# A long convolution beside a feed-forward block on one core: tying the order of TensorE's two streams to the program's, moving loads of the last stage, and a longer pause ahead of it

## The chip, the core and the metric

The kernel runs on one core of a Trainium2 chip. The metric is the device time of one execution in microseconds; the kernel before was run three times: 1074.57, 1076.01 and 1077.52 us, median 1076.01. A separate, profiled execution gives the trace that is read here.

The engines are named as the profile has them: PE is TensorE's matmuls and PEld its weight loads, DVE is VectorE, ACT is ScalarE, POOL is GpSimd, and SP is SyncE, which issues most of the DMAs (SPq, its queue). Each engine works through its own instructions in the order in which the built program has them. L685 is line 685 of the kernel's file.

## What is computed

The reference adds three parts for a sequence of 2048 rows and 576 columns (cut here to what matters):

```python
x = A_q
xn = layernorm(x)
k_shift = sum of 4 shifted k, each times shift_k     # short causal convolution
kv = k_shift * v
y = irfft(rfft(kv, 4096) * rfft(ssm_k, 4096))[:2048] # long causal convolution, per column
y = y + kv * ssm_D
ffn = relu(xn @ w1) @ w2                              # 576 -> 4608 -> 576
return x + xn * y + ffn
```

## The kernel before

Two streams of work share the engines, and both need TensorE.

**The feed-forward block (FFN)** goes through 18 pairs of 128-wide slices of the hidden width, twice: the first half of the program for rows 0 to 1023, the second half for the others. A visit computes the hidden values of 512 rows (`mm1`, L559, in the first half; `quad`, L587, in the second, with fewer products and more sums, whose partial results go through ScalarE and VectorE and back into PSUM) and puts them through `relu` (tiles `hh` and `ll`, the high and low part of each value, by ScalarE and VectorE). A `unit` (L616) multiplies hidden values by the second weights into a PSUM tile `pso`; VectorE adds it to `acc` (L636, L640). Units wait in a list, and `fill` takes two size units of them (24 matmuls) after each stage of a visit. GpSimd splits weights (`split_lo`, L426).

**The convolution (conv)** is a transform by matrices in four stages, written as a generator, `conv` (L694), which hands control back after each piece of work:

- fk: 64 steps transform `ssm_k`. For a step, VectorE transposes a block (`tr`, L758, one for two steps), ScalarE and VectorE split it into the stacked operand `ks` (L678, L679), TensorE multiplies it by `wk` (two matmuls, L685), ScalarE copies the result (`zk`, L686) and a DMA stores it. `ks`, `wk` and the copies have three buffers each.
- fx: 64 steps do the same for the gated `k * v`, with operands `xs` that are put together by DMAs (L839).
- fm: 192 steps, the middle of the transform and the product of both spectra; it ends with stores into `zy`.
- fo: 64 steps transform back, four for each of 16 row tiles. Each two steps need a load `zo` of 576 KB from `zy` (L991; four buffers, asked for three loads ahead). For each row tile, `load_rest` (L994) loads the matrix `wi` (GpSimd's queue, L998), the rows `xt` (L160) and, for half of the tiles, the FFN's finished sums `ft` (L1004, two buffers). `gate` and `add` (L1012, L1020) combine them on VectorE.

**What sets the order.** While the program is written out, each group of FFN matmuls calls `tick` with its columns (the moving operand's width, a measure of TensorE's work). `tick` lets the conv generator go on when its share is due: each piece has a cost (`W_FK`, `W_FX`, `W_FM`, `W_FO`) and `rate` spreads all of them over the FFN's columns; a negative yield is a pause of so many columns. That gives the program's order. But the built order on each engine is made by a scheduler that plays the program through with its own durations: whenever an engine is free, it takes the earliest instruction of the program whose operands are ready by its reckoning. So an FFN matmul can go ahead of a conv step that stands earlier in the program, and the other way round. `tc.issue_after(a)` forbids that for the instructions inside the block: on their engine they come behind `a`. It adds no wait on a semaphore; it only fixes an order. `here` (L689) uses it for conv's work on VectorE and ScalarE. Nothing used it for matmuls.

Of the kernel before, what the change touches and what calls it, by code (L numbers as in the profile page):

```python
# [10 lines left out]
F32 = mybir.dt.float32  # L11
# [6 lines left out]
P = 128  # L18
S = 2048
D = 576  # L20
# [3 lines left out]
NH = D // 2  # L24
# [10 lines left out]
HT = T // HALVES  # L35
# [25 lines left out]
W_QUAD = sum(W_STAGE)  # L61
FFN_TOTAL = NPAIR * HB * (W_PLAIN + W_QUAD + 2 * 4 * W_UNIT)
# [47 lines left out]
def h3_ffn_kernel(ctx: ExitStack, tc, x, k, v, shift_k, ssm_k, ssm_D, w1, w2, fwd, inv, mid, out):  # L110
    nc = tc.nc
# [35 lines left out]
    acc = {}  # L147
# [52 lines left out]
    done = {}  # L200
# [339 lines left out]
    def bank(m, name):  # L540
        return ps_h.tile([P, 512], F32, tag=f"h{m}", name=name)

    def run_seq(ps, seq, start=False):
        for i, (a, m) in enumerate(seq):
            nc.tensor.matmul(ps, a, m, start=start and i == 0, stop=i == len(seq) - 1,  # L545
                             skip_group_check=not start)

    def relu(n, s, j, ps):
        hh = hp.tile([P, 512], F32R, tag="hh", name=f"hh{n}_{s}_{j}")
# [10 lines left out]
    def mm1(n, s, j):  # L560
        g = weights[n][j]
        ps = bank(j, f"psh{n}_{s}_{j}")
        seq = []
        for c in range(4):
            b = ops[s, "b2" if c % 2 else "b1"][:, :, c // 2]
            seq += [(g[:, 0, c], b[:, 0]), (g[:, 0, c], b[:, 1]), (g[:, 1, c], b[:, 0])]
        seq += rest(n, j, s)
        for i, (a, m) in enumerate(seq):
            nc.tensor.matmul(ps, a, m, start=i == 0, stop=i == len(seq) - 1)  # L569
            if i % 7 == 6:  # L570
                tick(W_PLAIN / 4)
        relu(n, s, j, ps)
# [42 lines left out]
    def unit(ns, s, b, i, h, last):  # L615

        t = b * BT + i
        cols = slice(i * P, (i + 1) * P)
        final = b >= HB and last
        if final:  # L620
            while t not in added:
                next(stream)
        ps = ps_o.tile([P, 512], F32, tag="o", name=f"pso{ns[0]}_{t}_{h}")
        dc = slice(h * NH, (h + 1) * NH)
        seq = []
        for n in ns:
            for j in range(FT):
                hh, ll = hid[n, s, j]
                w = weights[n]["w2", h][:, :, j]
                seq += [(hh[:, cols], w[:, 0]), (hh[:, cols], w[:, 1]), (ll[:, cols], w[:, 0])]  # L630
        for c, (a, m) in enumerate(seq):
            nc.tensor.matmul(ps[:, :NH], a, m, start=c == 0, stop=c == len(seq) - 1)  # L632
            if c % 6 == 5:
                tick(6 * NH)
        if b == 0:
            done["acc"] = nc.vector.scalar_tensor_tensor(  # L636
                acc[t][:, dc], ps[:, :NH], rstd[:, t:t + 1], acc[t][:, dc],
                op0=OP.mult, op1=OP.add)
        else:
            done["acc"] = nc.vector.tensor_tensor(acc[t][:, dc], ps[:, :NH], acc[t][:, dc],  # L640
                                                  OP.add)
# [39 lines left out]
    def first(w, stk, z, u):  # L681

        ps = fft_psum()
        for n in range(2):
            nc.tensor.matmul(ps[:, :NH], w[:, n, :], stk, start=n == 0, stop=n == 1)  # L685
        nc.scalar.activation(z, ps[:, :NH], AF.Copy)  # L686

    @contextmanager
# [6 lines left out]
    def conv():  # L695
# [179 lines left out]
        with tc.tile_pool(name="fm", bufs=2) as fp:  # L875
# [22 lines left out]
            def run(hi, lo, d, h):  # L898

                ps = fft_psum()  # L900
                cols = slice(h * NH, (h + 1) * NH)
                seq = [(m_sb[:, d, 0, :], hi), (m_sb[:, d, 0, :], lo), (m_sb[:, d, 1, :], hi)]
                for n, (a, m) in enumerate(seq):
                    nc.tensor.matmul(ps[:, :NH], a, m[:, cols], start=n == 0, stop=n == 2)
                return ps[:, :NH], cols

            load(zk, 0, "k")
# [69 lines left out]


        with tc.tile_pool(name="fo", bufs=2) as fp:
            parts, rest, ys = {}, {}, {}  # L980


            order = [*range(HT, T), *range(HT)]
# [10 lines left out]
            def load_rest(i):  # L994
                if i < T:
                    t = order[i]
                    w = fp.tile([P, U, P], F32R, tag="wt", name=f"wi{t}", bufs=3)
                    nc.gpsimd.dma_start(w, inv[t])  # L998
                    xt = fp.tile([P, D], F32, tag="xt", name=f"xt{t}", bufs=3)
                    move(xt, x, t)  # L1000
                    ft = None
                    if t < HT:
                        ft = fp.tile([P, D], F32, tag="ft", name=f"ft{t}", bufs=2)
                        nc.sync.dma_start(ft, fin[t // 2, :, t % 2, :])  # L1004
                    rest[i] = w, xt, ft

            def gate(i):

# [6 lines left out]
            def add(i):  # L1015
                if i >= 0:
                    t = order[i]
                    to, more = (ys[i], rest[i][2]) if t < HT else (acc[t], acc[t])
                    with here():
                        nc.vector.scalar_tensor_tensor(to, ys[i], rstd[:, t:t + 1], more,  # L1020
                                                       op0=OP.mult, op1=OP.add)
# [6 lines left out]
                load_z(n)  # L1028
            for i in range(2):
                load_rest(i)  # L1030
            yield -2 * PAUSE
            for n, (t, u) in enumerate(units):
                i = n // U
                w = rest[i][0]
# [5 lines left out]
                for h in range(2):  # L1040


                    ps = fft_psum()
                    cols = slice(h * NH, (h + 1) * NH)
                    nc.tensor.matmul(ps[:, :NH], w[:, u, :], hi[:, cols], start=True, stop=False)  # L1045
                    nc.tensor.matmul(ps[:, :NH], w[:, u, :], lo[:, cols], start=False, stop=True)  # L1046
# [194 lines left out]
```

## Time and profile before

| what | value |
|---|---|
| median of 3 runs | 1076.01 us |
| the profiled execution's own time | 1079.17 us |
| its span, first to last instruction | 1077.4 us |
| TensorE busy | 1054.3 us, 98% |
| VectorE, ScalarE, GpSimd busy | 742.6, 549.6, 396.9 us |
| mean granted clock of TensorE | 0.994 |
| DMA | 204.45 MB, 190 GB/s |
| fk steps on TensorE | 82.4 to 205.4 us |
| fx steps | 238.6 to 503.3 us |
| fo steps | 891.5 to 1042.9 us |

A busy TensorE in this profile is one with a matmul under way; what counts is where it is not, and what ended that. A view by stretches gives, for each stretch of time, the busy time of each engine, the number of instructions, the granted clock (1.00 is full), the DMA engines' busy share and GB/s. The waits name the instruction that waited, what it waited for, the total, how often, and the longest. The chain is followed back from the last instruction through whatever released each step.

### The profile page before, as it was taken

The numbers are of one execution on the slowest core, as the hardware profiler recorded it, in microseconds if no ns is written. First come the engines' busy times: TensorE is split into PE (matmuls) and PEld (weight loads), VectorE is DVE, ScalarE is ACT, GpSimd is POOL, SyncE is SP. The second block draws the span as 40 slices with busy tenths as digits, with TensorE's granted clock in tenths as the row PEclk, the third lists the DMA queues.
The fourth block names the chain that finished last, engine by engine and source line by source line (L and its number), as shares of the span: only waits on it lengthen the run. The fifth ranks groups of instructions, "written<-read, shape, count | busy, mean of one in ns | idle before, by whom it ended". The sixth has DMA issues, their size and how long they took to land. (4 is left out here: it accounts for less than half of the span.)

```text
span 1077.4 us, 20001 instructions
## 1 busy us (share of the span) xinstructions
PE 1054.3 (98%) x7153; PEld 992.8 (92%) x7153; DVE 742.6 (69%) x1314; ACT 549.6 (51%) x1201; POOL 396.9 (37%) x398
## 2 busy tenths in 40 slices
PE   8999999999899999999999999999999998999998
PEld 5889999998799999999999999999999998999897
DVE  4539778779686878752487778777877755665654
ACT  4226556434433444432477787778677753443330
POOL 4133333232223233334343544434343444444531
PEclk9999999999999999999999999999999999999999
DMA  8845867778756766856875565566565559766824
GB/s 205 199 95 143 221 174 212 196 220 213 207 175 173 200 157 194 249 154 199 292 226 183 175 176 178 168 190 179 168 192 143 156 167 317 235 222 198 265 67 110
DMA packets 156303, 204.45 MB, mean 190 GB/s; under 512 B 32845, under 2 KB 122703, under 8 KB 155180
## 3 DMA queue, kind: packets, MB, share of 16 engines
q1 hardware_dynamic: 143308, 189.00, 59.3%
q0 software_dynamic: 12576, 13.44, 5.6%
q8 instruction: 56, 0.92, 0.4%
q10 hardware_dynamic: 320, 0.74, 0.3%
q14 instruction: 43, 0.35, 0.1%
HBM read 133.92 MB, written 55.05 MB: 175 GB/s over the span
## 5 line engine op out<-in xcount | busy, mean ns | idle before, releaser
L632 PE MATMUL pso<-w,hh 128*128 128x288 f32 x2304 | 470.5, 295 | 1.6 <-ACT w L531 0.8
L632 PEld LDWEIGHTS pso<-w,hh 128*128 128x128 f32 x2304 | 373.7, 188 | 10.3 <-ACT w L531 1.2
L632 PE MATMUL pso<-w,ll 128*128 128x288 f32 x1152 | 328.1, 295 | 0.0
L427 POOL TENSOR_TENSOR g<-r,g 128x256 fp32r<-128x256 f32 (+2 forms) x145 | 169.4, 1174 | 385.0 <-ACT g L469 343.8
L569 PE MATMUL psh<-b,g 128*128 128x512 f32 x864 | 218.9, 397 | 0.5 <-ACT b L223 0.2
L632 PEld LDWEIGHTS pso<-w,ll 128*128 128x128 f32 x1152 | 212.9, 188 | 1.0
L569 PEld LDWEIGHTS psh<-b,g 128*128 128x128 f32 x864 | 158.1, 189 | 31.1 <-DVE b L224 0.5
L640 DVE TENSOR_TENSOR acc<-pso,acc 128x288 f32<-128x288 f32 x232 | 102.3, 450 | 73.8 <-PE pso L632 72.8
L427 POOL TENSOR_TENSOR w<-r,w 128x576 fp32r<-128x576 f32 x72 | 115.2, 1601 | 57.8 <-ACT w L531 57.6
L551 ACT ACTIVATE hh<-psh 128x512 fp32r<-128x512 f32 x72 | 42.9, 597 | 127.1 <-PE psh L569 127.0
L552 DVE SCALAR_TENSOR_TENSOR ll<-psh,hh 128x512 fp32r<-128x512 f32 x72 | 49.3, 685 | 69.2 <-ACT hh L551 68.7
L545 PE MATMUL psb<-t,g 128*128 128x256 f32 x648 | 95.8, 281 | 0.0
L469 ACT ACTIVATE g<-r 128x256 fp32r<-128x256 f32 (+2 forms) x145 | 76.2, 542 | 33.6 <-DMA r<-in_w 25.4
L545 PEld LDWEIGHTS psb<-t,g 128*128 128x128 f32 x648 | 86.2, 189 | 0.1
L498 POOL TENSOR_TENSOR r<-r 128x256 f32<-128x256 f32 x72 | 58.0, 826 | 37.4 <-DMA r<-in_w 36.1
L545 PE MATMUL psa<-b,g 128*128 128x256 f32 x432 | 63.0, 281 | 0.4 <-ACT psa L596 0.4
L545 PE MATMUL psb<-b,g 128*128 128x256 f32 x432 | 59.6, 284 | 0.0
L545 PEld LDWEIGHTS psa<-b,g 128*128 128x128 f32 x432 | 56.6, 188 | 0.6 <-ACT psa L596 0.6
L545 PEld LDWEIGHTS psb<-b,g 128*128 128x128 f32 x432 | 56.0, 192 | 0.1
L672 POOL DMA_DIRECT2D wx<-in_fwd x32 | 17.7, 555 | 96.8 <-PE psf L685 85.6
L551 ACT ACTIVATE hh<-psa 128x512 fp32r<-128x512 f32 x36 | 21.6, 599 | 58.0 <-PE psa L545 57.7
L636 DVE SCALAR_TENSOR_TENSOR acc<-pso,rstd,acc 128x288 f32<-128x288 f32 x72 | 36.4, 510 | 20.1 <-PE pso L632 19.6
(134 smaller groups left out, 1693.7 us busy)
## 6 DMA issues: line engine op xcount, KB each, us to landing
r<-in_w SPq DMA_DIRECT2D x72, 288.0 KB, 3.6
zy<-vo SPq DMA_DIRECT2D x64, 288.0 KB, 3.1
zo<-zy SPq DMA_DIRECT2D x32, 576.0 KB, 5.8
r<-in_w SPq DMA_DIRECT2D x35, 512.0 KB, 4.5
zk<-zk SPq DMA_DIRECT2D x64, 144.0 KB, 2.5
ztk<-zk SPq DMA_DIRECT2D x32, 288.0 KB, 3.2
ztx<-zx SPq DMA_DIRECT2D x32, 288.0 KB, 3.1
k<-k SPq DMA_DIRECT2D x64, 144.0 KB, 3.2
```

The source lines that it names most:

```text
L427: return nc.gpsimd.tensor_tensor(dst, src, hi, OP.subtract)
L469: nc.scalar.activation(hi, src, AF.Copy)
L498: nc.gpsimd.tensor_tensor(dst, a, b, op)
L545: nc.tensor.matmul(ps, a, m, start=start and i == 0, stop=i == len(seq) - 1, skip_group_check=not start)
L551: done["act"] = nc.scalar.activation(hh, ps, AF.Relu)
L552: lows.append(nc.vector.scalar_tensor_tensor(ll, ps, 0.0, hh, op0=OP.max, op1=OP.subtract))
L569: nc.tensor.matmul(ps, a, m, start=i == 0, stop=i == len(seq) - 1)
L632: nc.tensor.matmul(ps[:, :NH], a, m, start=c == 0, stop=c == len(seq) - 1)
L636: done["acc"] = nc.vector.scalar_tensor_tensor(acc[t][:, dc], ps[:, :NH], rstd[:, t:t + 1], acc[t][:, dc], op0=OP.mult, op1=OP.add)
L640: done["acc"] = nc.vector.tensor_tensor(acc[t][:, dc], ps[:, :NH], acc[t][:, dc], OP.add)
L672: nc.gpsimd.dma_start(w, src)
```

## The change

1. **The order of matmuls.** Conv's matmuls in fk, fx, fm and fo now stand behind the last FFN matmul that was written before them (`done["pe"]`). FFN matmuls stand behind the newest conv step that is at least `LAG` = 4000 FFN columns old (`in_turn`). So an FFN matmul may pass a conv step by about 4000 columns, and a conv step passes no FFN matmul that was the last one written. FFN matmuls keep their freedom among themselves. Since `tick` comes every 1728 to 4096 columns, the limit is met in such pieces.
2. **Loads of fo.** `load_rest(i + 2)` is called one step later (in the first step of a tile's second half, instead of the second of its first half). The load of `ft` leaves it and becomes `load_sum(i)`, for the tile at hand instead of two tiles ahead; it is called behind the `add` of two tiles before, which frees its buffer.
3. **The pause ahead of fo** is 13/4 of 16,000 columns instead of 2; the sum of all pauses, `PAUSES`, grows by the same 1.25, so the rest of conv runs at a rate that is 1.2% higher.

```diff
+LAG = 4000
-PAUSES = 4 * NH // Q // KB * KT_GAP / PAUSE + 14
+PAUSES = 4 * NH // Q // KB * KT_GAP / PAUSE + 15.25
...
+    steps = []
+
+    def in_turn():
+
+        before = clock["ffn"] - LAG
+        while len(steps) > 1 and steps[1][0] <= before:
+            steps.pop(0)
+        if steps and steps[0][0] <= before:
+            return tc.issue_after(steps[0][1].ins)
+        return nullcontext()
+
+    def step(ins):
+        steps.append((clock["ffn"], ins))
...
         for i, (a, m) in enumerate(seq):
-            nc.tensor.matmul(ps, a, m, start=i == 0, stop=i == len(seq) - 1)
+            with in_turn():
+                done["pe"] = nc.tensor.matmul(ps, a, m, start=i == 0, stop=i == len(seq) - 1)
...
     def first(w, stk, z, u):
 
         ps = fft_psum()
-        for n in range(2):
-            nc.tensor.matmul(ps[:, :NH], w[:, n, :], stk, start=n == 0, stop=n == 1)
+        with tc.issue_after(done["pe"].ins):
+            for n in range(2):
+                last = nc.tensor.matmul(ps[:, :NH], w[:, n, :], stk, start=n == 0, stop=n == 1)
+        step(last)
         nc.scalar.activation(z, ps[:, :NH], AF.Copy)
...
-                    ft = None
-                    if t < HT:
-                        ft = fp.tile([P, D], F32, tag="ft", name=f"ft{t}", bufs=2)
-                        nc.sync.dma_start(ft, fin[t // 2, :, t % 2, :])
-                    rest[i] = w, xt, ft
+                    rest[i] = w, xt
+
+            def load_sum(i):
+                t = order[i]
+                if t < HT:
+                    sums[i] = fp.tile([P, D], F32, tag="ft", name=f"ft{t}", bufs=2)
+                    nc.sync.dma_start(sums[i], fin[t // 2, :, t % 2, :])
...
-            yield -2 * PAUSE
+            yield -13 * PAUSE / 4
...
                     if h == 0:
                         load_z(n + 3)
+                        if u:
+                            load_rest(i + 2)
                     else:
                         (gate if u == 0 else add)(i - 1)
                         if u == 0:
-                            load_rest(i + 2)
+                            load_sum(i)
                     yield W_FO
```

The matmuls of `run_seq`, `unit`, fm (`run`) and fo are wrapped in the same way.

What this does to the built order is shown at three places. The number at a name's end counts tiles in the order in which the program asks for them; the same tile has nearly the same number in both kernels. `psh` is the PSUM tile of `mm1`, `psa` and `psb` are those of `quad`, `pso` that of a unit, `psf` that of a conv step. First, TensorE in fk, before, where conv's step for `ks5_1` stands:

```order
L569 MATMUL psh4_0_1_1535<-xr_0_369,g4_2_1368 128x512 x2
L632 MATMUL pso2_2_1_1576<-w2_2_1_945,hh2_1_0_772 128x288
L685 MATMUL psf_1318<-ks5_1_1285,wk10_1214 128x288 x2
L632 MATMUL pso2_2_1_1576<-w2_2_1_945,hh2_1_0_772 128x288
L632 MATMUL pso2_2_1_1576<-w2_2_1_945,ll2_1_0_773 128x288
L632 MATMUL pso2_2_1_1576<-w2_2_1_945,hh2_1_1_837 128x288 x2
L685 MATMUL psf_1342<-ks21_0_1307,wk11_1260 128x288 x2
L632 MATMUL pso2_2_1_1576<-w2_2_1_945,ll2_1_1_838 128x288
```

The conv step 1318 stood inside the FFN unit 1576: TensorE had gone far ahead in the FFN. The same step now:

```order
L706 MATMUL psf_1318<-ks5_1_1285,wk10_1214 128x288 x2
L651 MATMUL pso2_3_0_1376<-w2_3_0_991,hh3_1_0_941 128x288 x2
L651 MATMUL pso2_3_0_1376<-w2_3_0_991,ll3_1_0_942 128x288
L651 MATMUL pso2_3_0_1376<-w2_3_0_991,hh3_1_1_1079 128x288 x2
L651 MATMUL pso2_3_0_1376<-w2_3_0_991,ll3_1_1_1080 128x288
L706 MATMUL psf_1342<-ks21_0_1307,wk11_1260 128x288 x2
L587 MATMUL psh4_0_0_1412<-b1_0_367,g4_0_988 128x512 x3
L587 MATMUL psh4_0_0_1412<-b2_0_368,g4_0_988 128x512 x2
L706 MATMUL psf_1359<-ks21_1_1323,wk11_1260 128x288 x2
```

It stands inside unit 1376, close to its place in the program; two whole units and two `psh` tiles that were ahead of it are now behind. Over the stage, the last of the 64 fk steps moves from FFN column 371,712 to 294,176, the first stays at 139,584.

Second, TensorE in fo, before, at the loads `zo11` and `zo12`:

```order
L545 MATMUL psb31_0_11386<-t_0_5305,g31_2_11308 128x256 x6
L545 MATMUL psa31_0_11387<-b2_0_5710,g31_2_11308 128x256 x6
L545 MATMUL psa31_0_11387<-xr_0_5712,g31_3_11352 128x512 x2
L1045 MATMUL psf_11780<-zo11_11587,wi13_11500 128x288
L1046 MATMUL psf_11780<-zo11_11587,wi13_11500 128x288
L1045 MATMUL psf_11813<-zo11_11587,wi13_11500 128x288
L1046 MATMUL psf_11813<-zo11_11587,wi13_11500 128x288
L1045 MATMUL psf_11855<-zo12_11654,wi14_11630 128x288
L1046 MATMUL psf_11855<-zo12_11654,wi14_11630 128x288
L545 MATMUL psb31_0_11386<-t_0_5305,g31_3_11352 128x256 x6
```

Three conv steps stand in a row, ahead of FFN work that comes before them in the program. Now, behind the first step of `zo11`:

```order
L651 MATMUL pso30_10_1_11853<-w2_30_1_11251,hh30_0_0_11291 128x288 x2
L651 MATMUL pso30_10_1_11853<-w2_30_1_11251,ll30_0_0_11292 128x288
L651 MATMUL pso30_10_1_11853<-w2_30_1_11251,hh30_0_1_11339 128x288 x2
L651 MATMUL pso30_10_1_11853<-w2_30_1_11251,ll30_0_1_11340 128x288
L651 MATMUL pso30_10_1_11853<-w2_31_1_11610,hh31_0_0_11480 128x288 x2
L651 MATMUL pso30_10_1_11853<-w2_31_1_11610,ll31_0_0_11481 128x288
L651 MATMUL pso30_10_1_11853<-w2_31_1_11610,hh31_0_1_11516 128x288 x2
L651 MATMUL pso30_10_1_11853<-w2_31_1_11610,ll31_0_1_11517 128x288
L561 MATMUL psb32_1_11743<-t_1_5449,g32_2_11663 128x256 x6
```

A whole FFN unit and stages of the quad (the first row of one is shown) lie between the two steps of one load, where none lay before.

Third, SyncE in fo, before, at the loads `zo23` to `zo28`:

```order
L160 DMA xt3_12257<-in_x 64x576 x2
L443 DMA r1_34_12088<-in_w1 128x4x256
L445 DMA r1_34_12088<-in_w1 64x256 x2
L1004 DMA ft2_12144<-fin_89 128x576
L452 DMA r2_34_0_12185<-in_w2 128x2x288
L991 DMA zo23_12368<-zy_87 128x1152
L991 DMA zo24_12425<-zy_87 128x1152
L991 DMA zo25_12490<-zy_87 128x1152
```

`ft2`, asked for long before, stands ahead of a run of `zo` loads (six, up to `zo28`). Now:

```order
L1016 DMA zo22_12307<-zy_87 128x1152
L161 DMA xt3_12311<-in_x 64x576 x2
L1032 DMA ft2_12408<-fin_89 128x576
L453 DMA r2_34_1_12347<-in_w2 128x2x288
L1016 DMA zo23_12377<-zy_87 128x1152
L161 DMA xt4_12455<-in_x 64x576 x2
L1032 DMA ft3_12546<-fin_89 128x576
L1016 DMA zo24_12451<-zy_87 128x1152
```

`ft` and `xt` loads stand singly between the `zo` loads.

More of the change, by code (lines that the diff above doesn't have):

```diff
@@ L631, in unit @@
         for c, (a, m) in enumerate(seq):
[L632 removed]
+            with in_turn():
+                done["pe"] = nc.tensor.matmul(ps[:, :NH], a, m, start=c == 0,
+                                              stop=c == len(seq) - 1)
             if c % 6 == 5:
@@ L902, in run @@
                 seq = [(m_sb[:, d, 0, :], hi), (m_sb[:, d, 0, :], lo), (m_sb[:, d, 1, :], hi)]
-                for n, (a, m) in enumerate(seq):
-                    nc.tensor.matmul(ps[:, :NH], a, m[:, cols], start=n == 0, stop=n == 2)
+                with tc.issue_after(done["pe"].ins):
+                    for n, (a, m) in enumerate(seq):
+                        last = nc.tensor.matmul(ps[:, :NH], a, m[:, cols], start=n == 0,
+                                                stop=n == 2)
+                step(last)
                 return ps[:, :NH], cols
@@ L1017, in add @@
                     t = order[i]
-                    to, more = (ys[i], rest[i][2]) if t < HT else (acc[t], acc[t])
+                    to, more = (ys[i], sums[i]) if t < HT else (acc[t], acc[t])
                     with here():
```

16 lines of the change are left out of this document (11 added, 5 removed).

## The prediction

> **What bounds the kernel now.** I read the busy time by stage first, with cuts where the conv changes stage: kernel transform (fk), input transform (fx), middle (fm), output transform (fo).
>
> ```profile
> 75.00:210.00 135.00, 135.00 (x828) 123.70 (x827) 109.97 (x199) 77.88 (x180) 47.77 (x57) 1.00 0.65 180
> 210.00:300.00 90.00, 85.10 (x498) 76.61 (x497) 69.78 (x113) 35.10 (x69) 28.48 (x29) 0.98 0.76 210
> 550.00:875.00 325.00, 324.90 (x2484) 320.90 (x2483) 251.53 (x439) 240.31 (x539) 134.74 (x114) 1.00 0.58 174
> 875.00:1045.00 170.00, 162.59 (x1216) 159.55 (x1215) 100.18 (x187) 67.05 (x154) 80.21 (x90) 0.98 0.70 221
> sum 1077.40, PE 1054.31 PEld 992.80 DVE 742.57 ACT 549.59 POOL 396.86; mean PE 131.79 PEld 124.10 DVE 92.82 ACT 68.70 POOL 49.61
> ```
>
> The columns after the stretch are its length and the busy time of TensorE, weight load, VectorE, ScalarE, GpSimd, then granted clock. TensorE bounds it: 1054.3 of 1077.4 us. Its idle time is 4.9 us at the start of fx, 7.4 in fo (170.00 - 162.59), none in fk and 0.1 in fm; the rest (10.7) lies at the two ends and at the start of fm. Next, what TensorE waited for:
>
> ```profile
> PE psf L1045 <- DMA zo<-zy: 6.3, 4, 2.4
> PE psf L685 <- DMA xs<-both: 4.9, 2, 3.1
> PE psf L1045 <- ACT psa L596: 1.1, 1, 1.1
> ```
>
> (total, times, longest.) In fo it is loads of `zo`. The chain that ended last shows why (start, length, what):
>
> ```profile
> 981.44 1.26 DVE y L1020
> 982.72 0.34 SPq L1004
> 983.16 1.26 SPq L452
> 984.52 5.50 DMA zo<-zy
> 990.15 0.37 PE psf L1045
> ...
> 1012.75 7.65 DMA zo<-zy
> 1020.54 0.37 PE psf L1045
> ```
>
> SyncE's queue stood at the `ft` load (L1004), which waits for VectorE's add (L1020) to free its buffer; six `zo` loads stand behind it. Last, the clock around the gaps:
>
> ```profile
> 275.00:280.00 5.00, 4.39 (x17) 3.82 (x18) 3.21 (x6) 1.59 (x4) 0.00 (x0) 0.70 1.06 281
> 890.00:895.00 5.00, 3.86 (x30) 3.67 (x29) 1.73 (x4) 2.36 (x6) 1.84 (x2) 1.00 1.18 300
> 905.00:909.00 4.00, 4.00 (x22) 4.00 (x22) 0.45 (x1) 1.50 (x4) 0.83 (x2) 0.57 1.04 316
> 1021.00:1025.00 4.00, 4.00 (x21) 3.81 (x20) 1.53 (x3) 1.31 (x3) 0.00 (x0) 0.57 0.13 48
> ```
>
> After the longest waits the clock falls for some 3.4 us: 0.43 x 4 = 1.7 us of work lost at 905 and again at 1021. Around the 1.1 us gap at 890 it stays at 1.00.
>
> **The change, fo.** Two things made TensorE wait: steps in bursts, and `zo` queued behind `ft`. By the order, the columns between the last use of a `zo` buffer and the first use of the load that refills it are 14,080 at least before (7 of 28 under 20,000) and 30,080 at least now. The rate comes from fk, below: 2.19 columns per ns. So the shortest room grows from 6.4 to 13.7 us. A load takes:
>
> ```profile
> DMA to landing us min/median/max: 3.8/5.8/9.3
> ```
>
> 13.7 us cover even 9.3, with 4 left for the queue. `ft` still stands in SyncE's queue, ahead of `zo23` for one; but it is now issued after the add that frees its buffer was issued, so it should wait little. The three loads that are moved (landing time last):
>
> ```profile
> xt<-in_x SPq DMA_DIRECT2D x32, 144.0 KB, 4.0
> ft<-fin SPq DMA_DIRECT2D x8, 288.0 KB, 4.1
> wi<-in_inv POOLq DMA_DIRECT2D x16, 128.0 KB, 6.1
> ```
>
> `xt` and `wi` (GpSimd's queue) go from 7 to 6 steps ahead of use, `ft` stands 6 ahead. A step of fo is now 331,072 / 64 = 5173 columns, 2.4 us, so each has 14 us: no cost. The longer pause (13/4 instead of 2 units of 16,000 columns) gives the first loads 20,000 columns, 9 us, more behind fm's last store. I credit the whole 7.4 us and both clock losses, 3.4: **-10.8**. More can't be gained, since that is all the idle time of the stage; the other bound is +2.4, SyncE as late as before and one more wait like the longest in the `zo` row. What is late next in fo: nothing on TensorE by the table; VectorE is at 100 of 170 us.
>
> The Trainium skill (TensorE: Matmul & The Clock Gate, "HAM oscillation") says the clock is lost at idle gaps over about 3.4 us. None of these gaps is that long, so by it nothing is regained from the clock and the sum below would be -2.4; the rows at 905 and 1021 speak against it, and I go by them.
>
> **The change, fk.** Here a cost is added that the trace does not show yet. Before, the conv fell behind the program: by the order, the 64 fk steps lie over 232,128 FFN columns, and TensorE ran FFN matmuls while a step's operands were late, so it never idled. Now FFN may pass a waiting step by about 4000 columns only, and the same steps lie over 154,592: what was a harmless delay becomes a wait of TensorE, if the other engines can't keep this pace. What the engines did from the first step to the last, and in the 25 us in which VectorE was fullest:
>
> ```profile
> 82.40:205.40 123.00, 123.00 (x752) 112.51 (x751) 101.37 (x184) 73.26 (x169) 43.90 (x53) 1.00 0.67 185
> 75.00:100.00 25.00, 25.00 (x152) 22.71 (x151) 22.88 (x49) 12.47 (x29) 9.71 (x10) 1.00 0.48 131
> ```
>
> TensorE: 232,128 + 128 x 288 = 268,992 columns in 123.0 us, 2.19 per ns; now 191,456 columns, 87.5 us. VectorE's order holds 28 instructions fewer between first and last step: 6 `ll`, 2 plain and 8 scaled `acc`, 12 of the next block's preparation.
>
> ```profile
> L679 DVE TENSOR_TENSOR ks<-tr,ks 64x288 fp32r<-64x288 f32 x62 | 35.9, 578 | 13.5 <-ACT ks L678 11.1 <-PE psf L685 0.5 <-PE pso L632 0.3
> L758 DVE STREAM_TRANSPOSE tr<-both 128x288 f32<-128x288 f32 x31 | 21.9, 708 | 0.6
> L552 DVE SCALAR_TENSOR_TENSOR ll<-psh,hh 128x512 fp32r<-128x512 f32 x16 | 10.8, 676 | 1.3 <-ACT hh L551 0.9
> L640 DVE TENSOR_TENSOR acc<-pso,acc 128x288 f32<-128x288 f32 x21 | 9.4, 452 | 2.4 <-PE pso L632 2.1
> L636 DVE SCALAR_TENSOR_TENSOR acc<-pso,rstd,acc 128x288 f32<-128x288 f32 x16 | 8.2, 510 | 1.9 <-PE pso L632 1.6
> ```
>
> 6 x 0.68 + 2 x 0.45 + 8 x 0.51 + 12 x about 0.6 (an estimate between these means) = 16.3; 101.4 - 16.3 = 85.1 us against TensorE's 87.5. VectorE would be 97% full where it was 82%, and 92% (22.88 of 25) at most with TensorE unbroken. The load is uneven. How many `ks` VectorE made in its first 25 us (the stretch's row for line 679 alone):
>
> ```profile
> 75.00:100.00 25.00, 6.15 (x11) 1.00 0.48 131
> ```
>
> Eleven; now 25 us at 87.5 / 64 = 1.37 us a step are about 18. Seven more at 0.58 + 0.71 / 2 = 0.93 make 22.9 + 6.5 = 29.4 us in 25: 4.4 too many. The rest, 85.1 - 29.4 = 55.7 in 62.5 us, is 89% and fits. Against the 4.4 stands a lead: operands are ready before TensorE takes them. Here is VectorE's last instruction for one step, and that step on TensorE:
>
> ```profile
> 98.95 0.45 DVE L679 TENSOR_TENSOR ks<-tr,ks 64x288 fp32r<-64x288 f32 x1
> ```
>
> ```profile
> 101.76 0.43 PE L685 MATMUL psf<-ks,wk 128*128 128x288 f32 x2
> ```
>
> The operand is ready at 99.40, 2.4 us before use. On the other side, VectorE is never 100% full: at 95%, the 29.4 us would take 31, 6 too many, less the lead 3.6, and some more for a second such place. I take **+5**; bounds 0 (lead and slack take it all; TensorE is busy in 135.00 of 135.00 us here, so nothing can be gained) and +15.8: VectorE stays as full as it was, 85.1 / 0.824 = 103.3 us, less 87.5. Behind a waiting conv step stand TensorE's FFN matmuls, and behind those VectorE's own `acc` and `ll`.
>
> **The rest.** In fx the steps stand where they did (step 4 at FFN column 463,136 in both orders; step 12 at 505,952 and now 505,664), so its 4.9 us and its clock loss (0.30 x 5 = 1.5) stay; bounds -6.4 and +2. In fm the steps stand on average 8000 columns earlier against the program, 3.6 us; no wait there now, VectorE at 77% (251.5 of 325): 0, bounds 0 and +3. FFN's own matmuls wait for nothing new: each sum still goes through the same three banks, and between a stage of the quad and the next there is still at least one unit of 24 matmuls in the program. The two ends of the kernel are not touched. Sum: -10.8 + 5 = **-5.8**. The profiled execution took 1079.17 (span 1077.4, 1.8 around it) and would take 1073.4; the runs' median is 1076.0, 3.2 below it, so 1070.2.
>
> **Rivals.** *Nothing is lost in fk* (chance 0.20). For it: the 2.4 us lead; against: 97% full. -10.8: 1065.2; with fx's waits gone as well, 1058.8.
> *VectorE holds fk* (0.20), the slower side: conv and FFN wait for each other in turn, so that VectorE idles as often as before and stays at 82%, +15.8 - 10.8 = +5.0: 1081.0. It decides from a stall of 10.8 us, a fullness of 85.1 / 98.3 = 87%. For it: 11.1 us of waits for ScalarE in the `ks` row, which a fuller queue need not remove; against: the 92% stretch.
> Some `ks` take far longer than the median (shortest, median, longest in ns), by about as much as one of GpSimd's splits lasts (mean ns behind the busy time):
>
> ```profile
> L679 DVE TENSOR_TENSOR ks<-tr,ks x64: 451/454/2198, 79.1 to 201.5; 64x288 fp32r<-64x288 f32 x64
> L427 POOL TENSOR_TENSOR g<-r,g 128x256 fp32r<-128x256 f32 (+2 forms) x145 | 169.4, 1174 | 385.0 <-ACT g L469 343.8 <-PE pso L632 22.3 <-DMA both<-in_k 8.5
> L427 POOL TENSOR_TENSOR w<-r,w 128x576 fp32r<-128x576 f32 x72 | 115.2, 1601 | 57.8 <-ACT w L531 57.6
> ```
>
> 62 x (578 - 454) ns = 7.7 us of such stretch are in VectorE's 101.4 already. The Trainium skill (SBUF — State Buffer, "Who interferes with whom") says that a VectorE instruction with two SBUF inputs and a GpSimd one that reads SBUF shut each other out, the later one for the whole of the earlier. By it alone the 17 GpSimd instructions that the order has in the stage could cost VectorE up to 7 x 1.60 + 10 x 1.17 = 22.9 us instead of the 7.7, 15 more, and the sum would be near this rival's; no run here shows so many collisions.
> *The change doesn't do in fo what it says* (0.13): SyncE's queue still comes late at half of the places, -5.4 + 5: 1075.6. For it: `ft` still stands ahead of `zo` loads; against: the doubled room.
> *The clock is not regained* (0.05): the idle time in fk comes in pieces as long as the 2.4 us in the `zo` row and the clock falls twice there, +3.4: 1073.6. Against: 1.1 us at 890 did nothing.
> *Forecast*: 0.42.
>
> **Numbers.** 0.3% (3.2 us) is about what a measurement of this kernel can tell from no change. Faster: the first rival, 0.20, and the forecast where the stall in fk is under 7.6 us (-10.8 + 7.6 = -3.2), 0.37 of its 0.42: 0.57. Same: the third and fourth rival, 0.18, and 0.03 of the forecast: 0.21. Slower: VectorE holds fk, 0.20, and the forecast's last 0.02, for a new wait in fm: 0.22. The range reaches from 1064 (no loss in fk, a little less in fx) to 1080 (most of the slower rival); outside lie both far ends, about 0.2.
>
> **What would show it.** Right: no `zo` wait among TensorE's, clock 1.00 through fo, and in fk TensorE idle for about 5 us, in its first third, ended by VectorE's `ks` or ScalarE, with VectorE over 90% busy. Wrong: fk unbroken (then some 1065), or fk over 98 us (then slower), or `zo` still in the list of waits.

## The result and the profile after

The changed kernel took 1082.15 us in the median of its six runs (1080.01 to 1085.17), the one before 1076.01: a ratio of 1.0064, 95% interval 1.0045 to 1.0083. It is slower by 0.64%. The profiled execution took 1081.85 us (span 1080.1); that of before had taken 1079.17, 3.2 above its median, so the two traces differ by 2.7 us where the medians differ by 6.1.

The changed kernel by the same stretches as before (length, busy TensorE, weight load, VectorE, ScalarE, GpSimd, granted clock):

```profile
75.00:210.00 135.00, 129.34 (x762) 115.44 (x761) 99.90 (x188) 74.40 (x173) 48.04 (x58) 0.99 0.71 193
210.00:300.00 90.00, 86.80 (x522) 78.62 (x521) 71.20 (x117) 35.64 (x70) 25.70 (x24) 1.00 0.66 181
...
550.00:875.00 325.00, 320.03 (x2433) 314.00 (x2432) 249.72 (x431) 238.10 (x534) 126.05 (x111) 1.00 0.59 176
875.00:1045.00 170.00, 168.89 (x1293) 166.08 (x1292) 103.51 (x194) 68.16 (x154) 84.90 (x95) 1.00 0.73 225
```

Idle TensorE (length less busy) went from 7.4 to 1.1 us in fo, with the clock back at 1.00, as forecast. It went from 0 to 5.7 in fk and from 0.1 to 5.0 in fm, and fell from 4.9 to 3.2 at the start of fx. What TensorE waited for, in total, times, longest:

```profile
PE psf L706 <- DVE ks L699: 4.7, 4, 2.4
PE psf L706 <- DMA xs<-both: 3.2, 1, 3.2
PE psf L927 <- DVE k L972: 2.3, 2, 1.4
PE psf L927 <- ACT k L960: 1.6, 3, 0.8
PE psf L927 <- DVE vo L985: 1.2, 2, 1.0
```

No `zo` is left; operands of fk (L706) and of fm (L927) stand in its place. By the steps, fk lasts from 82.3 to 179.5. Here are the stage as a whole, its three thirds, the 25 us from VectorE's first `ks` on, and the stretch in which VectorE was fullest before:

```profile
82.30:179.50 97.20, 91.77 (x545) 82.04 (x545) 81.36 (x155) 65.46 (x154) 34.84 (x47) 0.98 0.72 198
82.30:114.70 32.40, 30.50 (x185) 27.43 (x185) 30.99 (x67) 21.70 (x52) 12.26 (x16) 1.00 0.67 190
114.70:147.10 32.40, 31.22 (x187) 27.40 (x186) 26.89 (x46) 21.74 (x53) 11.79 (x16) 1.00 0.82 218
147.10:179.50 32.40, 30.04 (x178) 27.22 (x177) 23.48 (x44) 22.02 (x52) 10.78 (x17) 0.95 0.68 186
78.90:103.90 25.00, 24.55 (x149) 22.12 (x148) 22.79 (x54) 15.20 (x36) 8.05 (x10) 1.00 0.57 151
75.00:100.00 25.00, 24.55 (x152) 22.39 (x151) 22.67 (x49) 13.69 (x31) 10.15 (x11) 1.00 0.50 137
```

That is 97.2 us for 87.5 of columns at full rate: 9.7 lost. Of these, 5.4 are idle time of TensorE and 1.7 a stretch of half clock (its row is in the last section); behind a gap, the two matmuls of a step took 0.50 to 0.70 us where others take 0.43, and the rest is not accounted for. VectorE worked 81.4 of the 97.2 us, 84%: 96% in the first third, where TensorE idled 1.9 us, and 72% in the last, where it idled 2.4.

### The profile page after: what moved, and what is told of

The parts are those of the page before. It is cut to its first block, busy times and chain, and to the rows that moved or that the text cites. A ratio compares the mean times of both kernels' runs of the same rounds, so it can differ in the third digit from the quotient of the medians.

```text
span 1080.1 us, 19977 instructions
## 1 busy us (share of the span) xinstructions
PE 1056.1 (98%) x7153; PEld 989.6 (92%) x7153; DVE 740.0 (69%) x1314; ACT 550.8 (51%) x1201; POOL 390.2 (36%) x398
## 5 line engine op out<-in xcount | busy, mean ns | idle before, releaser
L651 PE MATMUL pso<-w,ll 128*128 128x288 f32 x1152 | 336.9, 295 | 0.2 <-DVE ll L569 0.2
L428 POOL TENSOR_TENSOR g<-r,g 128x256 fp32r<-128x256 f32 (+2 forms) x145 | 162.0, 1124 | 379.1 <-ACT g L470 300.3
L651 PEld LDWEIGHTS pso<-w,ll 128*128 128x128 f32 x1152 | 215.8, 188 | 1.5 <-DVE ll L569 0.4
L660 DVE TENSOR_TENSOR acc<-pso,acc 128x288 f32<-128x288 f32 x232 | 104.5, 452 | 81.9 <-PE pso L651 80.5
L568 ACT ACTIVATE hh<-psa 128x512 fp32r<-128x512 f32 x36 | 21.5, 598 | 65.4 <-PE psa L561 65.3
L692 POOL DMA_DIRECT2D wx<-in_fwd x32 | 17.5, 548 | 101.8 <-PE psf L706 89.9
```

Source lines behind the costliest of these rows:

```text
L428: return nc.gpsimd.tensor_tensor(dst, src, hi, OP.subtract)
L568: done["act"] = nc.scalar.activation(hh, ps, AF.Relu)
L651: done["pe"] = nc.tensor.matmul(ps[:, :NH], a, m, start=c == 0, stop=c == len(seq) - 1)
L692: nc.gpsimd.dma_start(w, src)
```

## The experiments

All have the loads and the pause of the changed kernel unless it is said otherwise. Where a part of the fixed order is taken out, it is by a switch over the stage names:

```diff
+PINNED = ("fo",)
...
-    def step(ins):
-        steps.append((clock["ffn"], ins))
+    def step(ins, stage):
+        if stage in PINNED:
+            steps.append((clock["ffn"], ins))
+
+    def behind(stage):
+        return tc.issue_after(done["pe"].ins) if stage in PINNED else nullcontext()
```

The table gives what they measured: the median, the ratio to the runs of before on the same chip with its interval, and TensorE's idle time by stretch in the profiled run, worked out as above.

| run | median us | ratio | fk 75-210 | fx 210-300 | fm 550-875 | fo 875-1045 |
|---|---|---|---|---|---|---|
| before | 1076.01 | 1 | 0 | 4.9 | 0.1 | 7.4 |
| after | 1082.15 | 1.0064 (1.0045-1.0083) | 5.7 | 3.2 | 5.0 | 1.1 |
| e1 order in fo | 1068.60 | 0.9935 (0.9914-0.9955) | 0 | 5.7 | 1.0 | 1.2 |
| e2 order in fk, fx, fm | 1083.75 | 1.0064 (1.0040-1.0087) | 5.7 | 2.5 | 4.9 | 1.0 |
| e3 no order | 1068.35 | 0.9926 (0.9906-0.9947) | 0 | 4.3 | 1.1 | 1.7 |
| e4 order only | 1086.70 | 1.0097 (1.0060-1.0133) | 6.0 | 2.9 | 5.8 | 0.8 |
| e5 order in fm | 1075.53 | 0.9988 (0.9972-1.0004) | 0 | 4.6 | 5.3 | 1.2 |
| e6 order in fk | 1076.94 | 1.0004 (0.9986-1.0021) | 7.6 | 1.9 | 0.7 | 1.9 |
| e7 loads only | 1071.67 | 0.9958 (0.9944-0.9973) | 0 | 4.2 | 0.2 | 3.6 |
| e8 pause only | 1068.53 | 0.9928 (0.9906-0.9950) | 0 | 4.7 | 0.9 | 1.7 |
| e9 LAG 12,000 | 1088.20 | 1.0101 (1.0074-1.0128) | 12.9 | 1.9 | 4.9 | 0.6 |
| e10 LAG 100,000 | 1066.01 | 0.9901 (0.9882-0.9920) | 0 | 4.8 | 0.7 | 0 |
| e11 slow fk | 1081.40 | 1.0046 (1.0029-1.0062) | 2.9 | 0 | 4.5 | 1.3 |
| e12 pause ahead of fx | 1069.20 | 0.9930 (0.9909-0.9950) | 0 | 0.9 | 0.3 | 4.7 |
| e13 LAG 40,000 | 1079.14 | 1.0027 (1.0010-1.0044) | 9.5 | 1.6 | 0 | 0 |
| e14 no ks on VectorE | 1080.12 | 1.0037 (1.0017-1.0058) | 3.2 | 3.1 | 4.7 | 1.0 |
| e15 LAG 100,000, e12's pauses | 1061.99 | 0.9864 (0.9840-0.9888) | 0 | 1.4 | 0.3 | 0 |
| e16 no split, 4000 | 1073.89 | 0.9980 (0.9962-0.9998) | 5.3 | 2.4 | 1.9 | 0 |
| e17 no split, 12,000 | 1074.04 | 0.9975 (0.9959-0.9991) | 8.2 | 0.6 | 3.8 | 0 |
| e18 no split, 100,000 | 1060.49 | 0.9854 (0.9826-0.9881) | 0 | 1.1 | 0.5 | 0 |

**Which part does what (e1 to e4).**

> The fixed order in the output transform alone; the other three stages are left to the scheduler as before; loads and pause as in the changed kernel. Before is at 1076.0, the changed kernel at 1082.2. Theory (the fixed order costs about 10 us in the key transform and 7 in the middle, and removes 10 in the output transform): 1066, from 1064 to 1069; TensorE without a wait longer than 1 us at 75 to 210 us and at 550 to 850, and no wait for zo. Rival A (the cost does not come from the order, but from the shifted dates and the moved loads): 1080 to 1084, with waits for ks and k as in the changed kernel. Rival B (a conv that lags in the middle also spoils the output transform, fixed order or not): 1072 to 1078.

> The fixed order in the key, input and middle transforms, not in the output transform; loads and pause as in the changed kernel. Theory (the order costs 10 us in the key transform and 7 in the middle; the gain of 10 in the output transform needs the order there): 1088 to 1092, with waits for zo among TensorE's. Rival (the moved loads and the longer pause alone clear the output transform): 1081 to 1084, no wait for zo.

e3 has `PINNED = ()`:

> No fixed order at all; only the moved loads and the longer pause. Theory: the waits for ks and k are gone, those for zo remain, though shorter, since the load that blocked the queue is issued later: 1070 to 1076. Rival (the loads and the pause bring the whole gain): 1065 to 1068, clock 1.00 through the output transform. Rival (they bring nothing): 1076 to 1079.

e4 keeps the order and takes back the loads and the pause:

```diff
-PAUSES = 4 * NH // Q // KB * KT_GAP / PAUSE + 15.25
+PAUSES = 4 * NH // Q // KB * KT_GAP / PAUSE + 14
...
+                    if t < HT:
+                        sums[i] = fp.tile([P, D], F32, tag="ft", name=f"ft{t}", bufs=2)
+                        nc.sync.dma_start(sums[i], fin[t // 2, :, t % 2, :])
                     rest[i] = w, xt
...
-            yield -13 * PAUSE / 4
+            yield -2 * PAUSE
...
-                        if u:
-                            load_rest(i + 2)
...
-                            load_sum(i)
+                            load_rest(i + 2)
```

> The fixed order in all stages, with the loads and the pause of the kernel before. Theory (the order brings the gain in the output transform by spreading its steps, the moved loads little): 1082 to 1085. Rival (the gain there comes from the moved loads): 1088 to 1092 with zo waits as before. Both have the waits for ks and k in the two earlier stages.

The order in fo is worth nothing beside the loads and the pause: e1 and e3 agree, and e2, without it, is as slow as the changed kernel, and all that its TensorE waited for `zo` is once 0.2 us. So the theory was right that the order costs time in fk and fm, and wrong that the gain in fo needs it: loads and pause bring 8.0 us (0.0074 of 1076). Yet with loads and pause of before (e4) the order clears fo too. Either is enough, so their gains do not add. The order in fk, fx and fm costs 0.0138, 14.8 us, give or take 3.

**Where the order costs (e5, e6), and loads against pause (e7, e8).** `PINNED = ("fm",)` and `("fk",)`:

> The fixed order in the middle alone; loads and pause as in the changed kernel. The same kernel with no fixed order took 1068.4. Theory (the order's cost of some 14 us lies about 10 in the key transform and 7 in the middle, less 3 regained in the input transform): 1074 to 1077, waits for k, vo and yl of some 7 us at 550 to 875 us, none for ks. Rival (the waits in the middle are late only because the key transform fell behind earlier; fixed in the middle alone the order costs nothing): 1067 to 1070.

> The fixed order in the key transform alone; the rest as in the run before this one. Theory: 1074 to 1079, waits for ks of 4 to 5 us at 75 to 210 us, one of them so long that the clock falls behind it. Rival (the cost is in the middle, what the key transform waits for is caught up before the end): 1067 to 1071.

e7 has `PAUSES` and the pause of before, e8 the loads of before (e4's edits to the loads), both with no order:

> No fixed order, the pause and rate of the kernel before, only the loads of the last stage moved. Theory now (SyncE's queue was held by the load of the earlier result behind VectorE's add, so moving that load is the whole gain): 1067 to 1070. Rival (the gain comes from the longer pause, which gives the first loads more time and shifts the steps against the rest): 1073 to 1077, waits for zo as before.

> No fixed order, loads as in the kernel before, only the longer pause and the rate that goes with it. Theory now (the moved loads are the gain): 1074 to 1078, with zo waits of 4 us or more in the last stage. Rival (the pause is the gain): 1067 to 1070, no zo wait over 1 us.

Against e3 the order in fm costs 0.0062, 6.7 us, and in fk 0.0078, 8.4 us, each give or take 3. Each stage waits alone much as it does in the changed kernel (in e6, 1.6 us more are for a load of `wk`). Both rivals fall. My reading of fo fell as well: the pause alone brings all of it, the loads some 4.5 us. TensorE's `zo` waits, loads only:

```profile
PE psf L1078 <- DMA zo<-zy: 3.1, 2, 2.0
```

and pause only:

```profile
PE psf L1075 <- DMA zo<-zy: 1.0, 1, 1.0
```

With the loads alone, the longer of the two is the wait at the start of the stage (904 us), which the pause removes; the other (1015 us) is left in both runs. SyncE still waits for the add at the `ft` load in the run with the pause alone:

```profile
SPq L1033 <- DVE y L1049: 21.2, 6, 7.2
```

But only one `zo` behind it comes late, by 1.0 us.

**How far a step may lag (e9, e10, e13) and the pace (e11).** `LAG = 12000`, `100000`, `40000`; for e11:

```diff
-W_FK, W_FX, W_FM, W_FO = 1.3, 4.65, 1.55, 2.35
+W_FK, W_FX, W_FM, W_FO = 1.8, 4.65, 1.55, 2.35
...
-PAUSES = 4 * NH // Q // KB * KT_GAP / PAUSE + 15.25
+PAUSES = 4 * NH // Q // KB * KT_GAP / PAUSE + 13.11
...
-                yield -9 * PAUSE / 2
+                yield -47 * PAUSE / 20
```

> The changed kernel with 12,000 columns in place of 4000 (8000 more, 3.6 us). The changed kernel took 1082.2, without its order 1068.4. Theory (short blocks of other work on VectorE, up to 3 us each, stand ahead of the key transform's operands, and 4000 columns leave no time for them): waits for ks under 3 us in total, for k, vo and yl under 3; 1071 to 1075. Rival (VectorE is full throughout, so the lag fills up and stays full): the waits in the key transform fall by 3.6 us at most, to 7 or so; 1077 to 1080.

> The changed kernel with 100,000 columns: a late conv step never holds TensorE's other matmuls, but a step still can't go ahead of its place. Theory (the cost comes from holding the others back): no waits for ks or k, 1067 to 1070. Rival (the cost comes from steps that may no longer run early, or from the added waits themselves): over 1075.

> The changed kernel, its order fixed within 4000 columns everywhere, with the key transform spread over 215,872 columns instead of 191,456 (98.6 instead of 87.5 us at full rate), taken from the pause behind it; VectorE would be about 90% full there instead of 97%. Theory (VectorE's fullness sets the wait): waits of 2 to 4 us instead of 10 at 75 to 210 us, 1074 to 1077. Rival (single blocks of VectorE's other work hold a step whatever the pace): 8 us or more remain, 1080 to 1083.

> The changed kernel with 40,000 columns. In the key transform the limit still binds in the second half (steps there were up to 82,432 columns late when left alone); in the other stages it binds nowhere (19,776 at most). With 4000 the kernel took 1082.2, with 12,000 1088.2, with 100,000 1066.0. Theory (as soon as the limit binds, steps stand in TensorE's order right where their operands are due, and every delay is a wait, however wide the limit is): waits for ks of 4 us or more, all behind the point where the limit is reached, 1071 to 1078; none in the middle. Rival (12,000 was a chance worst case, and waits shrink as the limit widens): waits for ks under 2 us, 1066 to 1069.

e10 settles that holding FFN matmuls behind late steps is the cost: without it fk and fm are as before, and the half that keeps steps from running early stays, harmless, with fo free of any wait. e9 was a surprise: both theories had a wider limit cheaper, and it was worse. e11 fits the theory in fk alone (2.9 us idle, and 4.9 us lost where it was 9.7: fk takes 103.5 us for 98.6); its time gained nothing, since fx got a new wait of 6.1 us for `xs` at 456 us, with half clock for the 4 us behind it. e13: with 40,000 columns the waits stand where the limit is reached, from 150 us on, and nowhere in fm; its median lies just above the range that its theory gave. Its profiled run (1072.4) is the lowest of its runs, so the idle time in the table is that of a better run than most. A limit that binds costs at each width tried.

**What makes the step late (e14, e16 to e18).** e14:

```diff
-        nc.scalar.activation(dst[own], src[own], AF.Copy)
-        nc.vector.tensor_tensor(dst[other], src[own], dst[own], OP.subtract)
+        nc.scalar.activation(dst, src, AF.Copy)
```

> The changed kernel (4000 columns) without VectorE's ks instruction: ScalarE writes all 128 rows of the operand in its one copy. Left out is the lower half of the key's split, so the key's transform is another one. VectorE loses 33 us of its 81 in the key transform, and TensorE's step follows ScalarE directly. Theory A (what comes late is ks in VectorE's queue, behind its other work): waits in the key transform of 1.5 us or less, 1069 to 1074. Theory B (the loop from a step over ScalarE's copies to the operand three steps on is too long, VectorE or not): 5 us or more remain at 75 to 210 us, 1077 to 1082.

e16 to e18:

```diff
-        return nc.gpsimd.tensor_tensor(dst, src, hi, OP.subtract)
+        return nc.gpsimd.memset(dst.bitcast(F32), 0.0)
```

> The changed kernel (4000 columns) with each of GpSimd's subtractions (the low halves of the FFN's weights) replaced by a memset of the same tile to zero, which reads nothing. Left out is the low half of the weights. TensorE's order stays the same to within a few hundred columns on average. In the changed kernel the ks of the key transform take 4.6 us more than at their shortest, and the longest waits fall where GpSimd works. Theory (GpSimd's subtractions stretch VectorE's instructions, and once the order leaves no lead, TensorE waits for that): at 75 to 210 us idle under 2.5 us instead of 5.7, no half clock; no ks over 600 ns; 1070 to 1076. Rival (the loop between the engines is late without them): idle over 4 us there, 1078 to 1082.

> The same with 12,000 columns, where the kernel with the subtractions idled for 12.9 us at 75 to 210 us and took 1088.2. Theory (stretched VectorE instructions): idle under 4 us, within 4 us of the run with 4000. Rival (VectorE's queue has acc, which waits for TensorE, ahead of ks, so both wait for each other without any stretch): 8 us or more remain.

> The same with 100,000 columns, as the yardstick: with the subtractions 1066.0, TensorE without a wait at 75 to 210 us. Without them, if they cost nothing where operands have a lead: 1062 to 1066, the gain only in the input transform and at the start. If it falls by more than 5 us, the subtractions cost time elsewhere too, and the two runs before are to be read against that.

e14 lies between its theories in idle time, and its 1080.1 us are Theory B's: with 27.6 us of VectorE's work gone (99.9 to 72.3), 3.2 us of idle time remain (135.00 less 131.82), and the time is lower than the changed kernel's by no more than the intervals allow:

```profile
75.00:210.00 135.00, 131.82 (x797) 118.97 (x796) 72.26 (x132) 68.69 (x177) 48.78 (x59) 1.00 0.74 201
```

2.6 of the 3.2 us are two waits of TensorE for ScalarE's copy `zk`, the first behind 3.48 us for which ScalarE stood at the store of an earlier result. The three with memsets separate two things. First, the stretched instructions. VectorE's `ks` in the changed kernel (shortest, median, longest ns):

```profile
L699 DVE TENSOR_TENSOR ks<-tr,ks x64: 451/453/1722, 78.9 to 176.6; 64x288 fp32r<-64x288 f32 x64
```

and with GpSimd's subtractions replaced:

```profile
L699 DVE TENSOR_TENSOR ks<-tr,ks x64: 451/453/455, 78.3 to 176.8; 64x288 fp32r<-64x288 f32 x64
```

They all go. With these two rows the rule of the Trainium skill (SBUF — State Buffer, "Who interferes with whom") that the prediction weighed agrees. The stretch explains much of fm (5.0 to 1.9 us idle) and part of the 12,000 case (12.9 to 8.2), but the sum in fk at 4000 hardly moves: 5.3 of 5.7 us remain. The theory falls there, and the rival, a loop between engines, stands; 12,000 lies just at its bound of 8. In time, e16 fell by 8.3 us, into the theory's range, but by e18 some 5 of these have nothing to do with the limit. So I read both against the runs with 100,000 columns. With the subtractions the limit costs 0.0163 (17.5 us) at 4000 and 0.0200 (21.5) at 12,000; without them 0.0126 (13.6) and 0.0121 (13.0), each give or take 3. The surplus of the 12,000 case over 4000 is gone, and most of the cost stays.

The gaps change too. The second-longest gap of the changed kernel in fk, in its first third:

```profile
106.23 2.28 DVE L192 TENSOR_SCALAR rows<-rows,mv,rstd 128x576 f32<-128x576 f32 x2
106.28 1.42 POOL L428 TENSOR_TENSOR w<-r,w 128x576 fp32r<-128x576 f32 x1
...
108.54 0.94 DVE L699 TENSOR_TENSOR ks<-tr,ks 64x288 fp32r<-64x288 f32 x2
...
109.05 0.54 PE L706 MATMUL psf<-ks,wk 128*128 128x288 f32 x2 [1.44 <-DVE ks L699]
```

ScalarE's part of that `ks` was ready at 106.13; VectorE, at work without a break, came to it at 108.54, since one `rows` took 1.80 us beside GpSimd's subtraction (the median is 0.57). In e16 the four `rows` take 0.57 to 0.58 us and 0.2 us of this gap remain; the idle time there lies elsewhere, the longest gap being 1.85 us ended by ScalarE's `zk`.

Second, that loop. What ScalarE's copy `zk` waited for in fk, before, after, and in e16 (three views):

```profile
ACT zk L686 <- PE psf L685: 17.0, 9, 3.1
...
ACT zk L686 <- DMA zk<-zk: 3.5, 4, 2.3
```

```profile
ACT zk L708 <- DMA zk<-zk: 10.0, 9, 2.2
ACT zk L708 <- PE psf L706: 8.1, 7, 1.9
```

```profile
ACT zk L708 <- DMA zk<-zk: 18.8, 17, 2.7
ACT zk L708 <- PE psf L706: 3.4, 6, 1.6
```

Before, the copy waited mostly for TensorE; now it waits most for the store of an earlier result to free one of its three buffers. In the other runs in which the limit binds it waited for the store 12.0 us (12,000 columns), 6.0 (40,000), 10.4 (slow fk), 19.4 (without `ks`) and 22.6 (e17), but 0.4 (e10) and 3.7 (e18) with 100,000. The first five don't rank with TensorE's idle time in fk (12.9, 9.5, 2.9, 3.2 and 8.2 us), so the store can't be the only link. What such a wait does is seen ahead of the longest gap of the changed kernel (timeline; in brackets the idle time before and what ended it):

```profile
157.61 0.41 ACT L708 ACTIVATE zk<-psf 128x288 f32<-128x288 f32 x1 [2.18 <-DMA zk<-zk]
...
158.05 0.44 ACT L698 ACTIVATE ks<-tr 64x288 fp32r<-64x288 f32 x1
...
158.52 0.45 DVE L699 TENSOR_TENSOR ks<-tr,ks 64x288 fp32r<-64x288 f32 x1 [2.61 <-ACT ks L698]
...
159.01 0.71 DVE L780 STREAM_TRANSPOSE tr<-both 128x288 f32<-128x288 f32 x1
...
159.64 0.66 DVE L569 SCALAR_TENSOR_TENSOR ll<-psh,hh 128x512 fp32r<-128x512 f32 x1
...
160.57 0.71 DVE L354 STREAM_TRANSPOSE rows<-rows 128x512 f32<-128x512 f32 x1
...
161.09 1.39 POOL L428 TENSOR_TENSOR w<-r,w 128x576 fp32r<-128x576 f32 x1
...
161.31 2.46 DVE L699 TENSOR_TENSOR ks<-tr,ks 64x288 fp32r<-64x288 f32 x3
...
162.85 0.70 PE L706 MATMUL psf<-ks,wk 128*128 128x288 f32 x2 [2.36 <-DVE ks L699]
```

ScalarE stands 2.18 us at `zk`, waiting for a store. The next `ks` stands behind it, VectorE waits 2.61 us for that, then makes up its arrears (`tr`, `ll`, `rows`), and three `ks` take 2.46 us in place of 1.36 while GpSimd subtracts. TensorE waits 2.36 us. In the 12,000 case the queue closes into a ring:

```profile
183.57 0.29 PE L651 MATMUL pso<-w,ll 128*128 128x288 f32 x1
...
183.90 0.52 DVE L656 SCALAR_TENSOR_TENSOR acc<-pso,rstd,acc 128x288 f32<-128x288 f32 x1 [1.07 <-PE pso L651]
...
184.34 1.44 DVE L364 TENSOR_TENSOR area<-rows,area 128x256 fp32r<-128x256 f32 x1
...
185.80 2.50 DVE L699 TENSOR_TENSOR ks<-tr,ks 64x288 fp32r<-64x288 f32 x3
...
187.39 0.85 PE L706 MATMUL psf<-ks,wk 128*128 128x288 f32 x2 [3.53 <-DVE ks L699]
```

VectorE stands 1.07 us at an `acc` that waits for TensorE's sum, and the `ks` for which TensorE then waits comes behind it. No store is in this one: ScalarE's part of that `ks` was ready at 184.27, 1.5 us before VectorE came to it. The room in `zk`'s ring by the trace: a step takes 87.5 / 64 = 1.37 us, three 4.1; the copy (0.41) and the store's median time to landing (2.7 in the changed kernel) fill 3.1 of it, and its longest landing is 6.7.

So the store begins the longest gap at 4000, VectorE's queue and GpSimd's stretch the second, and a wait for TensorE itself the longest at 12,000. What the store is worth is read from the traces, not tried: no run had more `zk` buffers. How much of the 9.7 us each link holds stays open.

**A better version (e12, e15).** e12 has no order, and e15 the order with `LAG = 100000`; both:

```diff
-PAUSES = 4 * NH // Q // KB * KT_GAP / PAUSE + 15.25
+PAUSES = 4 * NH // Q // KB * KT_GAP / PAUSE + 17.25
-                yield -9 * PAUSE / 2
+                yield -11 * PAUSE / 2
...
                     tap(1, n)
-                    yield -PAUSE / 4
+                    yield -PAUSE / 2
```

> No fixed order, moved loads and longer last pause, and two more units of pause ahead of the input transform, where TensorE still waits 4.2 us for xs with half a clock behind it; the rate of all steps rises for that. Theory (the first two tiles of the input transform have too little time): the waits for xs fall to 1 us or less, 1062 to 1065. Rival (their preparation is late by the key transform's own lateness of up to 82,432 columns, and the higher rate costs elsewhere): 1067 to 1070.

> 100,000 columns together with the longer pauses ahead of the input transform. With 100,000 columns alone 1066.0, of it 7.0 us of waits and half clock in the input transform; with the pauses and no fixed order 1.3 us there, but 5.8 in the output transform, against none with the fixed order. Theory (the two gains add, since the fixed order keeps the output transform's steps from running early): 1060 to 1063, no wait over 1 us at 210 to 300 us and none for zo. Rival (the higher rate makes zo late, order or not): 1065 to 1068.

In e12 fx came free (0.9), but fo idled more (4.7, three `zo` waits), which I put down to the higher rate; with the order and its limit at 100,000, e15 has both:

```profile
210.00:300.00 90.00, 88.57 (x528) 79.88 (x527) 72.98 (x117) 34.01 (x67) 29.38 (x28) 1.00 0.72 200
...
875.00:1045.00 170.00, 170.00 (x1304) 167.77 (x1303) 102.11 (x194) 67.11 (x154) 80.43 (x91) 1.00 0.74 220
```

It took 1061.99 us, 1.4% less than before, the fastest version that leaves nothing out.

## Why the prediction was wrong

**fo, -10.8: the size held in the main, the reason did not.** In the trace, idle time fell by 6.3 us and both stretches of half clock went (3.4); by the runs the loads and the pause bring 8.0. The prediction rested it on the shortest room between two loads growing from 14,080 to 30,080 columns. That is what the order does, and it was not needed: with the pause alone the shortest room is 14,368 columns and the gain is the same.

**fk, +5: a failed step, by its cause.** The prediction took VectorE for the limit, "97% full", and let the 2.4 us lead of the operands absorb the rest. VectorE had 81.4 us of work, less than the 85.1 reckoned, was busy 84%, and TensorE still lost 9.7 us by the trace and 8.4 by the runs (inside the term's bounds of 0 and +15.8). The overload on which the +5 rested was a misreading: the row with eleven `ks` begins 4 us ahead of VectorE's first one. Counted from that one, 25 us held 14 before and 15 after, not 11 and 18; VectorE was busy 22.8 of these 25 us, not 29.4, and TensorE idled 0.45. Further into the first third VectorE was full indeed, and there the second-longest gap lies; the longest lies at 160 us, in the last quarter, with VectorE at 72%. Not how full an engine was on the whole decided, but how links wait for each other: `zk` behind its store, `ks` behind `zk` on ScalarE, `ks` behind stretched or late work on VectorE. The rival "VectorE holds fk" came nearer: it had conv and FFN waiting for each other, VectorE's waits for ScalarE, and the 82%. That its time (1081.0) fits is in part luck: it had +15.8 in fk, where 8.4 were measured, and nothing in fm.

**fm, 0: the other failed step, and the larger in size.** It cost 6.7 us, outside its bounds of 0 and +3. The prediction itself had the steps 8000 columns, 3.6 us, earlier, and set against that only VectorE's mean of 77% and a stage without waits. A stage without waits had been one in which late steps were passed; its slack was the freedom that the change took, and with the limit at 100,000 the idle time there is 0.7 us again (5.0 with 4000; without GpSimd's subtractions 1.9). Which queue holds its operands up was not tried. The two steps, +8.4 and +6.7 in place of +5 and 0, with fo's -8.0, make +7 where the medians have +6.1.

**fx, 0**: idle 4.9 to 3.2 us; it was inside its bounds. e12 shows that a longer pause ahead of it would remove it.

**The clock**: one stretch of half clock came into fk, behind the 2.36 us gap, of the kind that the fourth rival named, and cost 1.7 us.

## What to carry over

Where the engine that bounds a kernel never waits in a stage, look at which operands were late there without harm before fixing its order: that freedom may be what hides them. Here a limit on lateness that binds turned delays into waits at 4000, 12,000 and 40,000 columns alike; the other side of the rule, that a step may not run early, cost nothing. And take a change of several parts apart before crediting its parts: here the pause alone had the whole gain.

## What the runs showed of the hardware

The clock after a gap is not told by the gap's length alone. In the changed kernel, the gap of 2.36 us in fk with what followed, and that of 3.20 at the start of fx (clock behind GpSimd's count):

```profile
160.40:162.80 2.40, 0.10 (x1) 0.00 (x0) 2.37 (x3) 2.16 (x6) 2.40 (x3) 1.00 0.35 123
163.10:166.40 3.30, 3.30 (x10) 2.62 (x10) 2.85 (x6) 0.85 (x2) 0.00 (x0) 0.50 0.90 242
280.60:283.80 3.20, 0.14 (x2) 0.00 (x0) 2.48 (x5) 1.02 (x2) 0.00 (x0) 1.00 1.17 304
283.90:287.30 3.40, 3.36 (x19) 3.03 (x20) 1.76 (x4) 1.64 (x4) 0.53 (x1) 1.00 1.06 292
```

The shorter gap halved the clock for 3.3 us, the longer did not. By the rule of the Trainium skill (TensorE: Matmul & The Clock Gate, "HAM oscillation"), that gaps over about 3.4 us lose the clock, neither should have; the rows agree for the second alone.

With the limit at 100,000 columns, GpSimd's subtractions cost TensorE no idle time in fk, though VectorE is busy for 110.2 us there with them and 98.8 without. The 1066.0 against 1060.5 us lie in fx: 4.8 against 1.1 us of idle time, and a clock of 0.98 against 1.00 over its 90 us.
